# A 64-channel remainder as 64-row matmuls in pairs, in a backward pass of 18 weight groups

## The chip, the cores and the metric

The kernel runs on one core of one Trainium2 chip. The metric is device time in microseconds (us) of one execution. The engines are TensorE (PE; its weight loads are PEld), VectorE (DVE), ScalarE (ACT), GpSimd (POOL) and SyncE (SP, which here only issues DMAs). Each executes its own instructions strictly in the order in which the program lists them.

## What is computed

The program is a layer and its gradients: `x + s * g` with a long convolution `s` (through Fourier transforms) and a gated feed-forward block `g`, and from `grad_out` the gradients of all inputs. L = 2048 tokens, D = 576 channels, F = 4608 hidden channels, bfloat16.

```
def _B_ref(x, w1, w3, w2):
    gate = jnp.einsum("bsd,df->bsf", x, w1)
    up = jnp.einsum("bsd,df->bsf", x, w3)
    h = _silu(gate) * up
    out = jnp.einsum("bsf,fd->bsd", h, w2)
    return out
...
xn = _layernorm(x, axis=-1)
s = _A_ref(xn, ...)            # y = irfft(rfft(u) * rfft(K)) + u * Dskip
g = _silu(_B_ref(xn, B_w1, B_w3, B_w2))
return x + s * g
```

The change concerns one product of the backward pass: the gradient by `h`, which is `go @ w2^T` with `go` the gradient by the feed-forward block's output (2048 x 576) and w2 (4608 x 576). Its inner dimension is D = 576 = 4 x 128 + 64.

## The kernel before

F is cut into 18 groups of 256 columns (`gi` 0 to 17), which run from about 645 to 1330 us; tokens are cut into 16 tiles of 128. In each group:

- `phase6_group` makes the gradient by `h` in four steps `s`. A step serves four token tiles: tiles 2s and 2s+1 of the first eight (j = 0) and the same of the last eight (j = 1), with one PSUM bank `ph` (pool `ps_h`, three banks) for each j. A tile takes five matmuls of 256 columns (L1936), one for each piece of 128 channels of `goT` against `w2T`. The fifth piece is `goTt`, whose rows 0 to 63 hold the 64 channels that remain and whose rows 64 to 127 are zero; `w2rows` is padded with zeros alike (L1690), and its transpose `w2T` comes by DMA (L1851). That is 80 matmuls in a group, 1440 in all, 288 of them the padded ones.
- ACT copies each bank to `gh` (L1939), and DVE multiplies `gh` into `gu_n` and `gg_n` (L1954: two products in a step, eight in a group).
- `phase6_grad2` makes the gradient by w2 (L1977, copies by ACT in L1983), `phase6_grad13` the gradients by w1 and w3 from `gu_n`, `gg_n` and `xn_bf` (L2002, then the 64 channels that remain as pairs of column halves in L2011 and L2013). `phase6_prep` prepares the next group on ACT (silu and its derivative, each with a table load) and DVE (L1900, L1901).

Beside groups 0 to 10 runs the backward convolution (`ssm_bwd_conv`): transforms on PE (L932), products of complex blocks on DVE (L963 to L971, into `Z`), the combination of two blocks into `ZZ` (L1453 on DVE), the inverse transform of `ZZ` on PE (L942, 16 matmuls for one ZZ, into two banks of the pool `et_ps` with three banks), scaled out of the banks by ACT and DVE (`gk_st`, L1470, L1473); and a second kind, from `Z` straight through PE (L952) with `gx` from ACT and DVE (L1500 to L1502). From group 11 on the parameter gradients take the convolution's place (L1537 on PE into `et_ps`, L1542 and L1545 on DVE).

The order on each engine is fixed when the program is built: the code emits operations with a due time (`self.at(us)`), and a scheduler picks by priority among those that are ready in its own reckoning. ACT's, SP's and POOL's operations of the groups are chained in the order in which they are emitted (`self.sc`, `self.sp`, `self.gp`). Pools hand out their banks in the order of the program too.

Of the kernel before, what the change touches and what calls it, by code (L numbers as in the profile page):

```python
# [13 lines left out]
FP32 = mybir.dt.float32  # L14
# [3 lines left out]
P = 128  # L18
# [82 lines left out]
class K:  # L101
    LEAD, SPAN, KG, TURN, TWICE = 1, 38, (4, 6.9), 34, 8
    SYNC = 13
    BACK = ((49, 0), (54, 0), (64, 2), (69, 1))

# [1056 lines left out]
    def ffn_output(self, T0, TB):  # L1162
# [9 lines left out]
        with ExitStack() as es:  # L1172
# [107 lines left out]
            def turn(i, after):  # L1280
                self.turn_go(i, pst.tile([P, DT, P], BF16, name="ptr"), after)

# [8 lines left out]
            product(second, F0, FT, last)  # L1291
            nc.gpsimd.memset(goTt[rem:P, :], 0.0)
            finish(first)
# [11 lines left out]
    def turn_go(self, i, ptr, after=None):  # L1305
        nc, cfg = self.nc, self.cfg
        nfull, rem = cfg.D // P, cfg.D % P
        for c, (do, dsz) in enumerate(cfg.dch):
            with self.tc.issue_after(after.ins) if after is not None else nullcontext():
                nc.tensor.transpose(ptr[0:dsz, c, :], self.go_o[:, i, do:do + dsz], self.ident_bf[:])  # L1310
        nc.scalar.copy(out=self.goT[:, :, i * P:(i + 1) * P], in_=ptr[:, 0:nfull, :])
        nc.scalar.copy(out=self.goTt[0:rem, i * P:(i + 1) * P], in_=ptr[0:rem, nfull, :])

# [67 lines left out]
    def conv_bwd_quarter(self, g, kp, zp, ps, T0, TQ):  # L1381
# [38 lines left out]
        for b in range(NB - 1, -1, -1) if g else range(NB):  # L1420
            self.at(T0 + (TQ * 0.05 * (NB - 1 - b) if g else 0))
            after = None
            if g == 0 and b == NB - 1:
                pt = ps.tile([P, 512], FP32, name="et_ps")
                self.turn_go(LT - 1, pt[:].bitcast(BF16)[:, 0:cfg.DT * P].rearrange("p (c t) -> p c t", t=P), self.dft_last)
                yield
                self.at(T0)
                after = self.pe_last
            G[b] = self.bgp.tile([P, 1, 2, KT, W], BF16, name=f"g_{b}")
            if g == 0:  # L1430
                folded = fold(slice(b, b + 1))
            if g == 0 and b == 0:
                after = first
            with self.tc.issue_after(after.ins) if after is not None else nullcontext():
                self.dft_folded(ps, self.cCS, (sums[b], gm[:, b]), G[b])
            if g == 0 and b == NB - 1:
                yield
# [225 lines left out]
    def backward(self, T0, TG, TQ, TC, TX, gctx, mats):  # L1663
# [11 lines left out]
        with ExitStack() as out:  # L1675
# [12 lines left out]
            self.w2rows = [rowp.tile([P, self.FG // P, cfg.DT * P], BF16, name=f"w2r{i}") for i in range(2)]  # L1688
            for w2r in self.w2rows:
                nc.gpsimd.memset(w2r[:, :, D:cfg.DT * P], 0.0)  # L1690
            with self.tc.issue_after(self.hc_loads[7].ins):
# [22 lines left out]
            self.at(T0)  # L1714
            group = self.phase6_group(0, cur, elp, gwp, ps_h, ps_gw)
            next(group)
# [32 lines left out]
            for gi in range(NG):  # L1749
# [9 lines left out]
                w2 = lambda g, fl: self.phase6_grad2(g, fl, hs[g], gwp, ps_gw)  # L1759
                for stage in group if gi == 0 else self.phase6_group(gi, cur, elp, gwp, ps_h, ps_gw):  # L1760
                    if stage == "h3" and self.chain and gi + 2 < NG:
# [63 lines left out]
    def w2row_load(self, gi):  # L1825
        D = self.cfg.D
        nfl = self.FG // P
        for fl in range(nfl):
            fi = gi * nfl + fl
            self.sp(lambda: self.nc.sync.dma_start(out=self.w2rows[gi % 2][:, fl, 0:D],  # L1830
                                                   in_=self.aps["B_w2"][fi * P:(fi + 1) * P, :]))

# [80 lines left out]

    def phase6_group(self, gi, tiles, elp, gwp, ps_h, ps_gw):
        nc, cfg = self.nc, self.cfg
# [4 lines left out]
        pair = lambda t_: t_[:].rearrange("p (j t) f -> p j t f", j=2)  # L1920
        made = {}

        def make(s):
            if gi == 0 and s == 3:
                gh = gwp.tile([P, 2, 2, FG], BF16, name="gh_3", tag="gw13")
            else:
                gh = elp.tile([P, 2, 2, FG], BF16, name="gh6")
            ph = [ps_h.tile([P, 2, FG], FP32, name="ph") for _ in range(2)]
            for k in range(2):
                t = s * 2 + k  # L1930
                for j in range(2):
                    tt = j * LH + t
                    steps = [(self.goT[:, c, tt * P:(tt + 1) * P], w2T[:, :, c, :]) for c in range(nfull)]
                    steps.append((self.goTt[:, tt * P:(tt + 1) * P], w2T[:, :, nfull, :]))
                    for n, (lw, rh) in enumerate(steps):
                        self.pe_last = nc.tensor.matmul(ph[j][:, k, :].rearrange("p (a f) -> p a f", f=P), lhsT=lw, rhs=rh,  # L1936
                                                        start=(n == 0), stop=(n == nfull))
            for j in range(2):
                self.sc(lambda: nc.scalar.copy(out=gh[:, j], in_=ph[j][:]))  # L1939
            made[s] = gh  # L1940
# [363 lines left out]
```

## Time and profile before

| what | value |
|---|---|
| three runs | 1632.05, 1639.41, 1641.4 us (median 1639.41) |
| span of the profiled execution | 1639.1 us |
| busy PE, DVE, ACT, POOL in that span | 1568.0, 1384.4, 837.0, 516.6 us |
| L1936, the product | 1440 matmuls, mean 273 ns of one |
| L1939, the bank copies | 144, mean 588 ns |

Times in the rows are us from the span's start. A row of a timeline has the start, the time until the last of its instructions ends, the engine, the line, out<-in, rows*columns of the weights, the tile's shape and the number of instructions that follow one another; in brackets the idle time before them and what ended it. Matmuls overlap, so a matmul's own duration (about 0.27 us here) is more than the distance from one to the next. A row of a table by stretches gives the stretch and its length, then busy us of PE, PEld, DVE, ACT and POOL with their instructions, the granted TensorE clock (1.00 is full speed), the DMA share and GB/s. A row of groups gives busy us and the mean ns of one after the bar, then the idle time before them with what ended most of it.

### The profile page before, as it was taken

To read this page: it belongs to the slowest core of one execution; us is meant where nothing else is said; L and a number is where in the kernel's file an instruction comes from. 1 tells how busy PE (TensorE), PEld (TensorE's weight loads), DVE (VectorE), ACT (ScalarE), POOL (GpSimd) and SP (SyncE) were. 2 spreads that over 40 slices of the span, in tenths; PEclk is the share of its full clock that TensorE was granted. 3 is DMA by queue.
4 is the path that set the end of the run, shared out by engine and by line. 5 is a ranking of instruction groups with operands and counts; after the bars stand their busy time and mean duration, and the time that the engine had idled before them with its cause. 6 is when DMAs were issued, how large, how long until landed. Compare 5 with 4: busy or idle time off the path is not lost. (4 is left out here: it accounts for less than half of the span.)

```text
span 1639.1 us, 34391 instructions
## 1 busy us (share of the span) xinstructions
PE 1568.0 (96%) x13331; PEld 1145.2 (70%) x13331; DVE 1384.4 (84%) x2145; ACT 837.0 (51%) x1520; POOL 516.6 (32%) x862
## 2 busy tenths in 40 slices
PE   6899999999999998999999999999999999999998
PEld 2454444444457776788888888888888887888786
DVE  8889998799965664998997999789999963988797
ACT  6989998766652114656556565565555411010011
POOL 7746765632352110111111011112122341515232
PEclk9999999999999999999999999999999999999999
DMA  7999999998999999676585766899999999999994
GB/s 236 346 345 363 374 346 382 369 268 257 320 287 214 240 200 205 182 216 202 176 246 156 213 190 183 226 240 264 247 272 223 244 254 241 240 216 215 237 241 88
DMA packets 616156, 408.26 MB, mean 249 GB/s; under 512 B 424698, under 2 KB 558426, under 8 KB 611386
## 3 DMA queue, kind: packets, MB, share of 16 engines
q1 hardware_dynamic: 561232, 277.45, 68.5%
q0 software_dynamic: 36576, 116.69, 22.2%
q10 hardware_dynamic: 18186, 11.95, 2.5%
q8 instruction: 104, 1.70, 0.4%
q14 instruction: 58, 0.48, 0.1%
HBM read 128.52 MB, written 188.76 MB: 194 GB/s over the span
## 5 line engine op out<-in xcount | busy, mean ns | idle before, releaser
L2002 PEld LDWEIGHTS <-xn_bf 128*128 128x128 bf16 x2304 | 224.3, 98 | 34.9 <-issue 8.7
L2056 PEld LDWEIGHTS <-acts 128*128 128x128 bf16 x1974 | 191.5, 98 | 52.3 <-DMA acts<-GG_dram 3.1
L1987 POOL DMA_DIRECT2D out_dram<-gw x72 | 47.2, 656 | 530.0 <-ACT gw L2004 313.8
L1542 DVE TENSOR_TENSOR pr_q<-et_ps,pz 128x1024 f32<-128x1024 f32 x144 | 175.8, 1221 | 28.7 <-PE et_ps L1537 21.0
L1123 PEld LDWEIGHTS <-xnT 128*128 128x128 bf16 x1152 | 107.9, 98 | 127.9 <-issue 20.9
L1545 DVE TENSOR_REDUCE S_all<-pr_q 128x32 f32<-128x1024 f32 x144 | 175.2, 1216 | 3.3
L1936 PE MATMUL ph<-w2T,goT 128*128 128x256 bf16 x1440 | 169.7, 273 | 1.5 <-ACT gh L1939 1.4
L1123 PE MATMUL pg<-wmB_w,xnT 128*128 128x512 bf16 x576 | 156.7, 381 | 1.1 <-DVE g_t L1142 0.6
L1977 PE MATMUL pgw<-go_o,h_n 128*128 128x288 bf16 x1152 | 152.4, 286 | 1.3 <-ACT gw L1983 1.0
L1936 PEld LDWEIGHTS <-goT 128*128 128x128 bf16 x1440 | 139.2, 98 | 18.7 <-issue 2.9
L1123 PE MATMUL pu<-wmB_w,xnT 128*128 128x512 bf16 x576 | 149.7, 379 | 0.0
L2056 PE MATMUL px<-wT,acts 128*128 128x288 bf16 x1134 | 145.8, 286 | 0.0
L2002 PE MATMUL pgw<-gu_n,xn_bf 128*128 128x256 bf16 x1152 | 133.3, 272 | 3.8 <-ACT gw L1983 3.3
L1977 PEld LDWEIGHTS <-h_n 128*128 128x128 bf16 x1152 | 111.9, 98 | 29.2 <-issue 2.1
L2002 PE MATMUL pgw<-gg_n,xn_bf 128*128 128x256 bf16 x1152 | 130.3, 273 | 0.4 <-ACT gw L2004 0.4
L1939 ACT CAST gh<-ph 128x512 bf16<-128x512 f32 x144 | 80.3, 588 | 82.9 <-PE ph L1936 76.5
L1138 ACT ACTIVATE s_t<-pg 128x512 bf16<-128x512 f32 x144 | 88.5, 614 | 55.8 <-PE pu L1132 43.2
L2179 ACT ACTIVATE go<-gx 128x576 bf16<-128x576 f32 x15 | 10.2, 683 | 195.3 <-DVE gx L2127 189.0
L813 POOL COPY KT<-k_s 64x128 bf16<-64x128 bf16 x144 | 84.5, 587 | 54.2 <-ACT k_s L810 49.5
L2056 PE MATMUL px<-wA,acts 128*128 128x288 bf16 x728 | 95.4, 286 | 4.4 <-DMA acts<-GG_dram 2.5
L1143 ACT CAST u_t<-pu 128x512 bf16<-128x512 f32 x144 | 87.5, 608 | 6.3 <-PE pu L1123 6.2
L1152 POOL DMA_DIRECT2D G_dram<-g_t x72 | 51.4, 715 | 119.0 <-ACT g_t L1140 91.1
(338 smaller groups left out, 3236.7 us busy)
## 6 DMA issues: line engine op xcount, KB each, us to landing
U_dram<-u_t POOLq DMA_DIRECT2D x72, 256.0 KB, 6.2
H_dram<-h_t SPq DMA_DIRECT2D x72, 256.0 KB
G_dram<-g_t POOLq DMA_DIRECT2D x72, 256.0 KB, 5.7
Q_dram<-q_k SPq DMA_DIRECT2D x36, 512.0 KB
GG_dram<-gg_n SPq DMA_DIRECT2D x36, 512.0 KB
GU_dram<-gu_n SPq DMA_DIRECT2D x36, 512.0 KB
gg_n<-G_dram POOLq DMA_DIRECT2D x14, 1024.0 KB, 6.6
E_dram<-E_k SPq DMA_DIRECT2D x54, 256.0 KB
```

The costliest lines, as they stand in the source:

```text
L813: nc.gpsimd.tensor_copy(out=KT[64 * hf:64 * hf + 64, :, ch // 9, h, d1:d1 + 8], in_=ks[64 * h:64 * h + 64, :, h, hf].rearrange("p d a -> p ...
L1123: ins = nc.tensor.matmul(pt[:], lhsT=xnT[:, c, ts], rhs=wm[w][:, c, :], start=(q == 0 and c == 0), stop=(q == 1 and c == nfull - 1))
L1138: nc.scalar.activation(out=s_t[:, :, q, :], in_=pgv, func=ACT.Silu)
L1143: self.gate_last = nc.scalar.copy(out=u_t[:, :, q, :], in_=puv)
L1152: self.u_stores[step] = nc.gpsimd.dma_start(out=dst[fb * ng:(fb + 1) * ng, :, i0:i0 + NT, :].rearrange("g p t f -> p g (t f)"), in_=src[:] ...
L1542: nc.vector.tensor_tensor(out=pr[:].rearrange("p r k e -> p r (k e)"), in0=T[x][:].rearrange("p z k h j a -> p (z k h j a)")[:, None].to_b ...
L1545: self.pr_last = nc.vector.tensor_reduce(out=self.S_all[:].rearrange("p r (h c) -> p r h c", h=2)[:, :, :, d0:d0 + 2], in_=pr[:].rearrange ...
L1936: self.pe_last = nc.tensor.matmul(ph[j][:, k, :].rearrange("p (a f) -> p a f", f=P), lhsT=lw, rhs=rh, start=(n == 0), stop=(n == nfull))
L1939: self.sc(lambda: nc.scalar.copy(out=gh[:, j], in_=ph[j][:]))
L1977: self.pe_last = nc.tensor.matmul(pgw[pi_][:, 0:pw], lhsT=hn[:, tt, fl * P:(fl + 1) * P], rhs=go_o[:, tt, po:po + pw], start=(tt == 0), st ...
L2002: self.pe_last = nc.tensor.matmul(pw_[:, 0:FG], lhsT=self.xn_bf[:, tt, c * P:(c + 1) * P], rhs=nat[:, tt, :], start=(tt == 0), stop=(tt == ...
L2056: self.pe_last = nc.tensor.matmul(px[pi_][:, 0:pw], lhsT=acts[i][:, ai, fi, :], rhs=w[:, po:po + pw], start=(n == 0), stop=(n == len(steps ...
```

## The change

The token tiles of j = 0 keep their 64 remaining channels in rows 0 to 63 of `goTt`, those of j = 1 go to rows 64 to 127, and the 64 channels of w2 are loaded twice, into both halves of the last piece of `w2rows`. The padded matmul becomes one of 64 rows, and the two of a pair (j = 0 and j = 1) use the two halves of the rows. The three memsets of zeros go; each `w2rows` block takes two DMAs instead of one (36 more on SP). In 15 groups two steps are made together: full pieces of the first tile of step s, those of step s+1, then four pairs of tails, then the full pieces of the second tiles. That needs four banks at a time: three `ph` and one `et_ps`. Groups 0, 2 and 8 (`LONE`) make each step alone, with two pairs in a run. `turn_go` puts the transposed tail, now a matmul with the identity, into its half of the rows.

```diff
@@ class K @@
+    LONE = (0, 2, 8)
...
-            nc.gpsimd.memset(goTt[rem:P, :], 0.0)
...
@@ -1305,11 +1305,16 @@
     def turn_go(self, i, ptr, after=None):
         nc, cfg = self.nc, self.cfg
         nfull, rem = cfg.D // P, cfg.D % P
-        for c, (do, dsz) in enumerate(cfg.dch):
-            with self.tc.issue_after(after.ins) if after is not None else nullcontext():
-                nc.tensor.transpose(ptr[0:dsz, c, :], self.go_o[:, i, do:do + dsz], self.ident_bf[:])
-        nc.scalar.copy(out=self.goT[:, :, i * P:(i + 1) * P], in_=ptr[:, 0:nfull, :])
-        nc.scalar.copy(out=self.goTt[0:rem, i * P:(i + 1) * P], in_=ptr[0:rem, nfull, :])
+        half, t = divmod(i, cfg.LT // 2)
+        r = slice(rem * half, rem * half + rem)
+        full = ptr[:].bitcast(BF16)[:, 0:nfull * P].rearrange("p (c t) -> p c t", t=P)
+        tail = ptr[r, 256:256 + P]
+        with self.tc.issue_after(after.ins) if after is not None else nullcontext():
+            for c in range(nfull):
+                nc.tensor.transpose(full[:, c, :], self.go_o[:, i, c * P:(c + 1) * P], self.ident_bf[:])
+            nc.tensor.matmul(tail, lhsT=self.go_o[:, i, nfull * P:cfg.D], rhs=self.ident_bf[:], start=True, stop=True)
+        nc.scalar.copy(out=self.goT[:, :, i * P:(i + 1) * P], in_=full)
+        nc.scalar.copy(out=self.goTt[r, t * P:(t + 1) * P], in_=tail)
 
     def ssm_bwd_conv(self, T0, TQ, ps):
         nc, cfg = self.nc, self.cfg
...
-            for w2r in self.w2rows:
-                nc.gpsimd.memset(w2r[:, :, D:cfg.DT * P], 0.0)
...
@@ -1827,8 +1830,9 @@
         nfl = self.FG // P
         for fl in range(nfl):
             fi = gi * nfl + fl
-            self.sp(lambda: self.nc.sync.dma_start(out=self.w2rows[gi % 2][:, fl, 0:D],
-                                                   in_=self.aps["B_w2"][fi * P:(fi + 1) * P, :]))
+            for o, d in ((0, 0), (D, D - D % P)):
+                self.sp(lambda: self.nc.sync.dma_start(out=self.w2rows[gi % 2][:, fl, o:o + D - d],
+                                                       in_=self.aps["B_w2"][fi * P:(fi + 1) * P, d:D]))
 
     def load_piece(self, wT, pool, tag, ai, f0, n):
         t = pool.tile([P, n, self.cfg.D], BF16, name=f"wT{ai}_{f0}", tag=tag)
@@ -1911,32 +1915,57 @@
                 products(sl)
             yield
 
-    def phase6_group(self, gi, tiles, elp, gwp, ps_h, ps_gw):
+    def phase6_group(self, gi, tiles, elp, gwp, ps_h, ps_gw, ps_b):
         nc, cfg = self.nc, self.cfg
         D, LT, FG = cfg.D, cfg.LT, self.FG
         nfull = D // P
         LH = LT // 2
         w2T, hn, gg, gu = tiles[0:4]
         pair = lambda t_: t_[:].rearrange("p (j t) f -> p j t f", j=2)
-        made = {}
+        made, phs = {}, {}
+        pairs = gi not in self.LONE
+        rem = D % P
+
+        def banks(s):
+            pools = (ps_h, "ph"), (ps_b, "et_ps") if pairs and s % 2 else (ps_h, "ph")
+            phs[s] = [pool.tile([P, 2, FG], FP32, name=name) for pool, name in pools]
+
+        def put(s, j, k, lhsT, rhs, start, stop, after):
+            with self.tc.issue_after(after.ins) if after is not None else nullcontext():
+                self.pe_last = nc.tensor.matmul(phs[s][j][:, k, :].rearrange("p (a f) -> p a f", f=P), lhsT=lhsT, rhs=rhs,
+                                                start=start, stop=stop)
+
+        def fulls(s, k, after):
+            for j in range(2):
+                tt = j * LH + s * 2 + k
+                for c in range(nfull):
+                    put(s, j, k, self.goT[:, c, tt * P:(tt + 1) * P], w2T[:, :, c, :], k == 0 and c == 0,
+                        k == 1 and c == nfull - 1, after if c == 0 else None)
+                after = self.pe_last
+
+        def tails(s, k):
+            t = s * 2 + k
+            for j in range(2):
+                r = slice(rem * j, rem * j + rem)
+                put(s, j, k, self.goTt[r, t * P:(t + 1) * P], w2T[r, :, nfull, :], k == 1, k == 0, self.pe_last)
 
         def make(s):
             if gi == 0 and s == 3:
                 gh = gwp.tile([P, 2, 2, FG], BF16, name="gh_3", tag="gw13")
             else:
                 gh = elp.tile([P, 2, 2, FG], BF16, name="gh6")
-            ph = [ps_h.tile([P, 2, FG], FP32, name="ph") for _ in range(2)]
+            run = (s, s + 1) if pairs and s % 2 == 0 else () if pairs else (s,)
+            after = None
+            for r in run:
+                banks(r)
+                fulls(r, 0, after)
+                after = self.pe_last
             for k in range(2):
-                t = s * 2 + k
-                for j in range(2):
-                    tt = j * LH + t
-                    steps = [(self.goT[:, c, tt * P:(tt + 1) * P], w2T[:, :, c, :]) for c in range(nfull)]
-                    steps.append((self.goTt[:, tt * P:(tt + 1) * P], w2T[:, :, nfull, :]))
-                    for n, (lw, rh) in enumerate(steps):
-                        self.pe_last = nc.tensor.matmul(ph[j][:, k, :].rearrange("p (a f) -> p a f", f=P), lhsT=lw, rhs=rh,
-                                                        start=(n == 0), stop=(n == nfull))
+                for r in run:
+                    tails(r, k)
+            fulls(s, 1, self.pe_last)
             for j in range(2):
-                self.sc(lambda: nc.scalar.copy(out=gh[:, j], in_=ph[j][:]))
+                self.sc(lambda: nc.scalar.copy(out=gh[:, j], in_=phs[s][j][:]))
             made[s] = gh
 
         if gi == 0:
```

The other edits pass the pool `ps` (the banks `et_ps`) to `phase6_group` and a bank of fp32 to `turn_go`. Line numbers of the changed kernel are higher: L1936 becomes L1935, L1939 L1968, L1954 L1983, L1977 L2006, L1983 L2012, L2002 L2031, L942 L943, L952 L953, L1453 L1458, L1473 L1478.

How the order changes is seen best in group 1. On PE of the kernel before, the ZZ with number 9300 is first read behind the group's last gradients (`pgw`, L2011 and L2013); `[waits DVE_49]` marks a wait for DVE:

```order
L2011 LDWEIGHTS xn_bf_103
L2011 MATMUL pgw_10008<-gg_n_9353,xn_bf_103 64x256
L2013 LDWEIGHTS xn_bf_103
L2013 MATMUL pgw_10008<-gu_n_9355,xn_bf_103 64x256
L942 LDWEIGHTS iT_6076
L942 MATMUL et_ps_9306<-ZZ_9300,iT_6076 128x144 [waits DVE_49]
```

All 80 matmuls of L1936 and the gradients of group 1 stand ahead of these rows. On PE of the changed kernel the same ZZ (now 9301) is read in two single matmuls ahead of group 1's first run, whose bank `et_ps_9671` is the first row of L1935 there:

```order
L943 MATMUL et_ps_9263<-ZZ_9246,iT_6076 128x144
L943 LDWEIGHTS iT_6076 [waits DVE_49]
L943 MATMUL et_ps_9307<-ZZ_9301,iT_6076 128x144 [waits PE_49]
L943 LDWEIGHTS iT_6076
L943 MATMUL et_ps_9321<-ZZ_9301,iT_6076 128x144 [waits PE_49]
L1935 LDWEIGHTS goT_6965
L1935 MATMUL et_ps_9671<-w2T_8883,goT_6965 128x256 [waits PE_49]
```

So the wait for that ZZ moved from behind group 1's work on PE to ahead of its 80 matmuls; the other 14 matmuls of that ZZ follow behind the product and the gradients. On DVE of the kernel before, the first products of group 1 (`gh6_9654`, `gh6_9681`) stand around the ZZ before that one (9245):

```order
L922 TENSOR_TENSOR gk_x_9246<-Z_9225,Z_9184 128x576
L1954 TENSOR_TENSOR gu_n_9355<-gh6_9654,gu_n_9355 128x2x512
L1453 TENSOR_TENSOR ZZ_9245<-gk_x_9246 128x2x288 x2
L1954 TENSOR_TENSOR gg_n_9353<-gh6_9654,gg_n_9353 128x2x512
L1954 TENSOR_TENSOR gu_n_9355<-gh6_9681,gu_n_9355 128x2x512
L1473 TENSOR_TENSOR gk_st_9152<-et_ps_9251,lcol_8931 128x18x8x2
L1954 TENSOR_TENSOR gg_n_9353<-gh6_9681,gg_n_9353 128x2x512
```

On DVE of the changed kernel the first product of group 1 (`gh6_9659`, L1983) stands behind the ZZ 9301, with nine rows of the next convolution block between:

```order
L970 TENSOR_TENSOR cm_t_10112<-g_2_9004,a2_0_9336 128x1152
L1458 TENSOR_TENSOR ZZ_9301<-gk_x_9302 128x2x288 x2
L964 TENSOR_TENSOR Z_9344<-g_3_9126,a2_0_9336 128x1152
L964 TENSOR_TENSOR Z_10110<-g_2_9004,a2_0_9336 128x1152
L971 TENSOR_TENSOR Z_9344<-Z_9344,cm_t_9346 128x576
L972 TENSOR_TENSOR Z_9344<-Z_9344,cm_t_9346 128x576
L971 TENSOR_TENSOR Z_10110<-Z_10110,cm_t_10112 128x576
L972 TENSOR_TENSOR Z_10110<-Z_10110,cm_t_10112 128x576
L967 TENSOR_TENSOR cm_t_10116<-g_3_9126,a2_1_9338 128x1152
L970 TENSOR_TENSOR cm_t_10119<-g_3_9126,a2_1_9338 128x1152
L968 TENSOR_TENSOR Z_10110<-Z_10110,cm_t_10116 128x1152
L1983 TENSOR_TENSOR gu_n_9358<-gh6_9659,gu_n_9358 128x2x512
```

All eight products of group 1 moved 27 rows or more down DVE's list, behind that ZZ. Groups 3 and 5 change in the same way: in group 3 the matmuls of two ZZ and the first two of a third, in group 5 the whole inverse transform of the next phase (34 matmuls of L943) stand ahead of the runs.

More of the change, by code (lines that the diff above doesn't have):

```diff
@@ L1280, in turn @@
             def turn(i, after):
-                self.turn_go(i, pst.tile([P, DT, P], BF16, name="ptr"), after)
+                self.turn_go(i, pst.tile([P, 512], FP32, name="ptr"), after)
             first = begin(0)
@@ L1424, in conv_bwd_quarter @@
                 pt = ps.tile([P, 512], FP32, name="et_ps")
-                self.turn_go(LT - 1, pt[:].bitcast(BF16)[:, 0:cfg.DT * P].rearrange("p (c t) -> p c t", t=P), self.dft_last)
+                self.turn_go(LT - 1, pt, self.dft_last)
                 yield
@@ L1714, in backward @@
             self.at(T0)
-            group = self.phase6_group(0, cur, elp, gwp, ps_h, ps_gw)
+            group = self.phase6_group(0, cur, elp, gwp, ps_h, ps_gw, ps)
             next(group)
@@ L1759, in backward @@
                 w2 = lambda g, fl: self.phase6_grad2(g, fl, hs[g], gwp, ps_gw)
-                for stage in group if gi == 0 else self.phase6_group(gi, cur, elp, gwp, ps_h, ps_gw):
+                for stage in group if gi == 0 else self.phase6_group(gi, cur, elp, gwp, ps_h, ps_gw, ps):
                     if stage == "h3" and self.chain and gi + 2 < NG:
```

## The prediction

> **What bounds the kernel now.** I read the page's busy times first, then the table by stretches, then the timelines of TensorE (PE) and VectorE (DVE) where the convolution runs beside the groups.
>
> ```profile
> span 1639.1 us, 34391 instructions
> ...
> PE 1568.0 (96%) x13331; PEld 1145.2 (70%) x13331; DVE 1384.4 (84%) x2145; ACT 837.0 (51%) x1520; POOL 516.6 (32%) x862
> L1936 PE MATMUL ph<-w2T,goT 128*128 128x256 bf16 x1440 | 169.7, 273 | 1.5 <-ACT gh L1939 1.4
> L2002 PE MATMUL pgw<-gu_n,xn_bf 128*128 128x256 bf16 x1152 | 133.3, 272 | 3.8 <-ACT gw L1983 3.3
> ...
> 700.00:740.00 40.00, 39.08 (x388) 33.90 (x386) 38.35 (x71) 22.86 (x40) 4.79 (x8) 1.00 0.76 217
> 860.00:900.00 40.00, 39.25 (x389) 33.73 (x388) 27.84 (x49) 25.19 (x48) 4.78 (x8) 1.00 0.52 160
> ```
>
> PE is the bound: 96% of the span, nearly all of these stretches (second number of a row). Less PE work could thus show in the time. But DVE is almost as full (38.35 of 40 us around 720). Whatever makes PE wait for DVE there costs directly, and the schedule of before is one in which PE always has other work while DVE computes.
>
> **The tails themselves.** The gate stage shows pairs of 64-row matmuls in this kernel, the plain column is L1936's run of 40 in group 1 (below).
>
> ```profile
> 303.20 0.81 PE L1123 MATMUL pu<-wmB_w,xnT 128*128 128x512 bf16 x3
> 303.94 0.39 PE L1132 MATMUL pg<-wtail,xnT 64*128 64x512 bf16 x1
> 304.17 0.38 PE L1132 MATMUL pg<-wtail,xnT 64*128 64x512 bf16 x1
> 304.48 0.29 PE L804 MATMUL kps<-v_k,q_k 128*128 128x64 bf16 x4
> ```
>
> Three full 512-column matmuls start at 303.20 and take 0.81 with a last one of about 0.38, so their pitch is 0.215 and the last starts at 303.63. The pair starts 0.31 later (0.097 over the pitch), the next pair 0.23 after it, and full rows 0.31 after that (again 0.096 over). With L1936's pitch of 0.109 ((4.53 - 0.273)/39 in the 40 matmuls at 696.14), a run of four pairs takes 0.206 + 3 x 0.120 + 0.205 = 0.77 from the last full start to the next, where eight padded matmuls and the next full one took 9 x 0.109 = 0.98: 0.21 saved. A run of two pairs takes 0.53 against 0.55. Thirty runs of four and twelve of two (groups 0, 2 and 8) give -6.6 us of PE at most.
>
> The Trainium skill ("TensorEngine Tiling (Array Packing)", Key Properties) says that a change of tiling mode drains TensorE, which speaks against short runs. Were each of the 84 switches to wait for the 0.38 that a row above lasts rather than 0.31, the saving would shrink by 84 x 0.07 = 5.6 us, to about 1; the starts above show a switch cheaper than that.
>
> How much of it is kept? Group 14 shows what ends a group's second run:
>
> ```profile
> 1193.72 1.09 ACT L1939 CAST gh<-ph 128x512 bf16<-128x512 f32 x2 [1.10 <-PE ph L1936]
> 1194.83 1.28 ACT L1904 ACT_TABLE_LOAD   x1
> 1197.08 0.38 ACT L1983 CAST gw<-pgw 128x288 bf16<-128x288 f32 x1
> ...
> 1197.52 0.71 PE L2002 MATMUL pgw<-gu_n,xn_bf 128*128 128x256 bf16 x5 [0.27 <-ACT gw L1983]
> ```
>
> The gradients (L2002) already wait for a ScalarE (ACT) chain: last gh copies, table load, silu, gw copy. After the change the four banks of steps 2 and 3 close together, so four copies of about 0.55 stand in a row behind the run and the chain does not start earlier. I give the second run of a group nothing and the first its 0.21: **-3 us**, between -6.6 (all kept) and 0.
>
> **Small parts.** Out go three POOL memsets (POOL is 32% busy and nobody waits: 0). The 16 tail transposes become matmuls of one row with the same number of columns, in a stage where PE waits for DMA: 0, within half a us. The 36 extra SP transfers stand in front of others in SP's queue; they matter where PE waits for SP's loads, at 632.89 (row below, 4.41 us): **+1**, between 0 and another 4.4.
>
> **The order, the large term.** A run now needs a fourth bank, which comes from et_ps, the pool that the convolution's inverse transform (L942, L943 after) uses. On PE all 80 matmuls of groups 1, 3 and 5 move behind that transform's first matmuls for the next operand ZZ (made by DVE, L1453), and with them everything behind: copies, DVE's gh products (L1954), gradients. Group 1 before:
>
> ```profile
> 692.28 0.30 PE L942 MATMUL et_ps<-ZZ,iT 128*128 128x144 bf16 x2
> 692.95 1.03 PE L942 MATMUL et_ps<-ZZ,iT 128*128 128x144 bf16 x14
> 696.14 4.53 PE L1936 MATMUL ph<-w2T,goT 128*128 128x256 bf16 x40
> 700.51 3.23 PE L1977 MATMUL pgw<-go_o,h_n 128*128 128x288 bf16 x25
> 704.00 1.91 PE L2002 MATMUL pgw<-gu_n,xn_bf 128*128 128x256 bf16 x16 [0.27 <-ACT gw L1983]
> 721.44 0.74 PE L942 MATMUL et_ps<-ZZ,iT 128*128 128x144 bf16 x9
> ...
> 692.81 0.68 DVE L1954 TENSOR_TENSOR gg_n<-gh,gg_n 128x1024 bf16<-128x1024 bf16 x1
> 693.41 0.68 DVE L1954 TENSOR_TENSOR gu_n<-gh,gu_n 128x1024 bf16<-128x1024 bf16 x1
> 710.60 1.42 DVE L1453 TENSOR_TENSOR ZZ<-gk_x 128x576 bf16<-128x576 f32 x2
> ...
> L1954 DVE TENSOR_TENSOR gg_n<-gh,gg_n 128x1024 bf16<-128x1024 bf16 x4 | 2.7, 683 | 0.0
> L1954 DVE TENSOR_TENSOR gu_n<-gh,gu_n 128x1024 bf16<-128x1024 bf16 x3 | 2.0, 682 | 0.0
> ```
>
> The last two rows group DVE's products from 692.5 to 703.5. DVE finishes the ZZ in question at 710.60 + 1.42 = 712.0, and PE needs it only at 721.44. After, that ZZ has no product ahead of it: seven at a pitch of 0.60 (692.81 to 693.41) fall out, 4.2 us, so its rows run from 706.4 to 707.8. PE gets there at about 694.5 (the 16 matmuls of L942 end at 692.95 + 1.03, a few of L1977 come with them) and has nothing else to issue: it waits some **12 us**. Then it does the two L943 (0.1), 80 matmuls with two runs (8.3) and 26 of L1977's kind (3.2), and the ACT chain takes its 0.3: the gradients start 11.9 later, at 719.7 instead of 704.00: **+15** (rounded down, since an eighth product moves behind as well). DVE cannot use the time: its next convolution rows need PE's L952 results of group 2, which are 15 later too.
>
> Group 3 is built alike; its third ZZ of the phase now stands ahead of the runs.
>
> ```profile
> 766.03 0.82 DVE L1453 TENSOR_TENSOR ZZ<-Z 128x576 bf16<-128x576 bf16 x2
> 789.68 1.42 DVE L1453 TENSOR_TENSOR ZZ<-gk_x 128x576 bf16<-128x576 f32 x2
> 783.12 1.91 PE L2002 MATMUL pgw<-gu_n,xn_bf 128*128 128x256 bf16 x16 [0.27 <-ACT gw L1983]
> ...
> L1954 DVE TENSOR_TENSOR gu_n<-gh,gu_n 128x1024 bf16<-128x1024 bf16 x4 | 2.7, 681 | 0.0
> L1954 DVE TENSOR_TENSOR gg_n<-gh,gg_n 128x1024 bf16<-128x1024 bf16 x4 | 2.7, 680 | 0.0
> ```
>
> From 766.03 to 789.68 DVE also does the group's eight products (last two rows, 766 to 789), 4.8 us at 0.60; without them the third ZZ comes 18.8 after the first, at 784.9 by the old clock, which is 15 late by now: 799.9. Two rows (1.4) and 11.9 later the gradients start, 813.2, 30 after 783.12: another **+15**.
>
> Group 5 takes the next phase's whole transform (34 matmuls of L943) ahead of its runs, which before lay in group 6:
>
> ```profile
> 850.44 1.16 PE L952 MATMUL et_ps<-Z,cT 128*128 128x144 bf16 x16 [0.91 <-DVE Z L970]
> 857.83 0.83 DVE L1453 TENSOR_TENSOR ZZ<-Z 128x576 bf16<-128x576 bf16 x2
> 858.50 0.71 PE L2002 MATMUL pgw<-gu_n,xn_bf 128*128 128x256 bf16 x5 [0.27 <-ACT gw L1983]
> ...
> 940.39 0.82 PE L2002 MATMUL pgw<-gu_n,xn_bf 128*128 128x256 bf16 x6 [0.18 <-ACT gw L1983]
> 1161.98 1.19 PE L2002 MATMUL pgw<-gu_n,xn_bf 128*128 128x256 bf16 x8 [0.27 <-ACT gw L1983]
> ```
>
> The first ZZ hangs on transforms behind the L952 at 850.44, 30 late: 887.8. The third follows 18.8 later (group 3's spacing), 906.6; plus 1.4 and 11.9 the gradients start at 919.9 instead of 858.50: 61 late, another **+30**. Some of it comes back: from 858.50 to 940.39 two groups took 81.9 us with that transform between them; without it group 6 is a plain one, and I take **-9**, between 0 and -11 (twice a group without convolution, 35.5 from 1161.98 to 1197.52). In groups 7 and 10 the L952 waits (0.91 at 850.44) lose the matmuls of L1936 that stood ahead of them, some 50 x 0.109 = 5.5 each, of which DVE, freed of a few products, gives back a part: **+7**, between 0 and 11. Laid end to end with these durations through PE, ACT and DVE, the rest of the groups shift alike.
>
> **The clock after a long wait.**
>
> ```profile
> 632.89 3.29 PE L1248 MATMUL po<-w2g,hcA 128*128 128x288 bf16 x16 [4.41 <-DMA hcA<-H_dram]
> 635.97 3.42 PE L1248 MATMUL po<-w2a,hcA 128*128 128x288 bf16 x22
> 639.23 0.56 PE L1310 MATMUL ptr<-ident_bf,go_o 128*128 128x128 bf16 x5
> ...
> 633.00:635.00 2.00, 2.00 (x12) 1.34 (x11) 0.00 (x0) 0.00 (x0) 0.00 (x0) 0.67 0.96 394
> 635.00:637.00 2.00, 2.00 (x10) 1.27 (x9) 0.99 (x2) 0.23 (x1) 0.00 (x0) 0.50 0.93 238
> ```
>
> After 4.41 us idle the granted clock (last but two) falls to 0.50 until 637, and the 38 matmuls take 6.34 us, where L1977's pitch ((3.23 - 0.286)/24 = 0.123) gives 4.66: 1.7 us lost. Of the long waits above four (groups 1, 3, 5, 10) have no further wait behind them that swallows it: **+7**, between 0 and twice that.
>
> **Sum:** -3 + 1 + 15 + 15 + 30 - 9 + 7 + 7 = +63. The profiled execution spans 1639.1 us, the median of three runs is 1639.41, so the same base: **1702 us**.
>
> **Rivals.**
> - *Only the first wait costs* (13 in 100). DVE's room between 860 and 900 (27.84 of 40 busy) says that it can run ahead; if the later ZZ are ready when PE comes, +15, the clock's 2 and the Z waits' 7 stay, less 3, plus 1: 1661. Against it: DVE's first rows of each phase need PE's results, so it is late with PE.
> - *More is late than PE and DVE* (12). The convolution's operands also come by DMA, which the walk takes as ready. A wait as at 632.89 (4.41 and 1.7) in each of five phases, once or twice, gives +30 to +60: 1730 to 1760.
> - *No wait: DVE has ZZ before PE asks, and the whole saving shows* (3). It decides from the point where DVE brings ZZ by 695 instead of 706, with under 3 us of its rows between the two ZZ, not 14. All runs then end early, the ACT chain with them, and L2002's 3.3 us of waits go as well: 1639.4 - 6.6 - 3.3 = 1629.5, faster by 0.6%.
> - *The change does little: runs' saving eaten by chain and banks, the order neutral* (4). 1639.4 - 3 + 1 = 1637.
>
> **How the numbers follow.** The forecast has 68 in 100, its own range 1672 to 1722: each group term may be a third smaller or the clock and Z terms double. Reaching down to the first rival's middle and a little over the top, 1660 to 1726 leaves out two in ten. A change under 0.5% (8 us, about what a measurement of this kernel can tell) needs the third or fourth rival: faster 0.02, same 0.05, slower 0.93.
>
> **What would show it.** Right: a wait of PE of 10 us or more in front of the runs in groups 1, 3 and 5, ended by DVE's ZZ row; granted clock near a half in the 3 us behind; L2031 at about 719, 813 and 920; groups from 12 on at the pace of before; pairs' members started together, 0.2 before and after. Wrong: PE busy through the runs of group 1, gradients there before 710, or DVE's ZZ row long done when PE arrives. The forecast falls if PE's instructions are not executed in the order shown, or if DVE's work between two ZZ is far shorter than the trace has them.

## The result, and the profile after

The changed kernel takes 1723.2 us in the median of four runs (1711.6 to 1740.5), the kernel before 1640.4: 1.048 times as long, 95% interval 1.043 to 1.053. Later runs on another occasion gave 1713.4 us and 1.042 (1.036 to 1.049). Ratios and their intervals, here and below, leave out the executions that lie over 1.5% above the fastest of the same kernel, among them that of the first profile of the changed kernel (1740.5 us), while the medians keep them. The first profile of the changed kernel spans 1738.7 us, the second 1702.5; where they differ is part of the explanation.

The page's head and the view of what TensorE waited for (us in total, times, longest), first profile:

```profile
span 1738.7 us, 34424 instructions
PE 1580.6 (91%) x13331; PEld 1133.7 (65%) x13331; DVE 1390.8 (80%) x2145; ACT 834.0 (48%) x1520; POOL 515.3 (30%) x859
...
PE et_ps L943 <- DVE ZZ L1458: 44.3, 11, 12.6
PE po L1249 <- DMA hcA<-H_dram: 28.6, 2, 27.9
PE et_ps L953 <- DVE Z L971: 14.5, 4, 5.2
```

PE's share fell from 96% to 91%, with nearly the same work. Three waits grew by 75.5 us together, most of the 99.6 us by which the span is longer: the inverse transform's for ZZ (2.7 us before), that for the load hcA ahead of group 0 (5.4 before, the longest piece 4.4), and the second transform's for Z (3.8 before). The timeline of PE in group 1, and the two ZZ rows of DVE:

```profile
717.83 0.30 PE L943 MATMUL et_ps<-ZZ,iT 128*128 128x144 bf16 x2
718.49 1.04 PE L943 MATMUL et_ps<-ZZ,iT 128*128 128x144 bf16 x14
732.11 0.42 PE L943 MATMUL et_ps<-ZZ,iT 128*128 128x144 bf16 x2 [12.59 <-DVE ZZ L1458]
732.33 1.06 PE L1935 MATMUL et_ps<-w2T,goT 128*128 128x256 bf16 x4
...
741.16 3.35 PE L2006 MATMUL pgw<-go_o,h_n 128*128 128x288 bf16 x26
744.81 1.91 PE L2031 MATMUL pgw<-gu_n,xn_bf 128*128 128x256 bf16 x16 [0.30 <-ACT gw L2012]
...
717.02 1.42 DVE L1458 TENSOR_TENSOR ZZ<-gk_x 128x576 bf16<-128x576 f32 x2
731.31 1.42 DVE L1458 TENSOR_TENSOR ZZ<-gk_x 128x576 bf16<-128x576 f32 x2
```

PE stands still from 719.5 to 732.1, until DVE has the next ZZ, then does the product (all but its first twelve matmuls, which came earlier) and only then the gradients. Counted from the last rows of group 0 (683.46 before, 709.0 after), the gradients of group 1 start at 35.8 instead of 20.5.

The distance of a group's first L2011 (L2040) from that of the group ahead, from the timelines, in us:

| group | before | changed, first profile | changed, second | difference (first) |
|---|---|---|---|---|
| 1 | 36.1 | 51.3 | 51.5 | +15.2 |
| 2 | 37.7 | 37.9 | 37.9 | +0.2 |
| 3 | 41.4 | 57.3 | 57.3 | +15.9 |
| 4 | 37.3 | 37.5 | 37.5 | +0.2 |
| 5 | 38.1 | 69.0 | 69.0 | +30.9 |
| 6 | 44.7 | 35.0 | 35.0 | -9.7 |
| 7 | 36.8 | 41.5 | 41.5 | +4.7 |
| 8, 9 | 42.0, 37.8 | 41.6, 39.5 | 41.6, 39.5 | +1.3 |
| 10 | 37.4 | 42.0 | 42.0 | +4.6 |
| 12 to 15 | 35.5 each | 35.7, 36.9, 35.7, 35.7 | 35.7, 35.7, 35.7, 36.7 | +0.2 each, two with a DMA wait |

Groups 1 to 10 together are 63.3 us longer. Where group 0's first of these rows lies is another matter: 683.5 before, 709.0 in the first profile, 683.2 in the second.

### The profile page after: what moved, and what is told of

It reads as the page before. It is cut to its first block, busy times and chain, and to the rows that moved or that the text cites. A ratio compares the mean times of both kernels' runs of the same rounds, so it can differ in the third digit from the quotient of the medians.

```text
span 1738.7 us, 34424 instructions
## 1 busy us (share of the span) xinstructions
PE 1580.6 (91%) x13331; PEld 1133.7 (65%) x13331; DVE 1390.8 (80%) x2145; ACT 834.0 (48%) x1520; POOL 515.3 (30%) x859
## 5 line engine op out<-in xcount | busy, mean ns | idle before, releaser
L2031 PEld LDWEIGHTS <-xn_bf 128*128 128x128 bf16 x2304 | 224.4, 98 | 36.7 <-issue 10.5
L1547 DVE TENSOR_TENSOR pr_q<-et_ps,pz 128x1024 f32<-128x1024 f32 x144 | 176.0, 1222 | 43.5 <-PE et_ps L1542 36.1
L2006 PE MATMUL pgw<-go_o,h_n 128*128 128x288 bf16 x1152 | 151.9, 286 | 2.3 <-DVE h_n L1905 1.4
L1935 PEld LDWEIGHTS <-goT 128*128 128x128 bf16 (+1 forms) x1440 | 122.2, 100 | 37.5 <-issue 21.8
L1935 PE MATMUL ph<-w2T,goT 128*128 128x256 bf16 (+1 forms) x1140 | 142.1, 281 | 0.6 <-ACT gh L1968 0.6
L2031 PE MATMUL pgw<-gu_n,xn_bf 128*128 128x256 bf16 x1152 | 133.0, 272 | 5.5 <-ACT gw L2012 4.0
L2006 PEld LDWEIGHTS <-h_n 128*128 128x128 bf16 x1152 | 111.9, 98 | 29.8 <-DVE h_n L1905 1.8
L2031 PE MATMUL pgw<-gg_n,xn_bf 128*128 128x256 bf16 x1152 | 130.3, 273 | 0.4 <-ACT gw L2033 0.4
L1968 ACT CAST gh<-ph 128x512 bf16<-128x512 f32 x114 | 60.7, 592 | 120.7 <-PE ph L1935 120.5
L1904 DVE TENSOR_TENSOR gg_n<-gg_n,h_n 128x1024 bf16<-128x1024 bf16 x72 | 48.7, 685 | 50.1 <-ACT gg_n L1911 48.2
```

Source lines behind the costliest of these rows:

```text
L1547: nc.vector.tensor_tensor(out=pr[:].rearrange("p r k e -> p r (k e)"), in0=T[x][:].rearrange("p z k h j a -> p (z k h j a)")[:, None].to_b ...
L1904: nc.vector.tensor_tensor(out=gg[:, sl, :], in0=gg[:, sl, :], in1=hn[:, sl, :], op=ALU.mult)
L1935: self.pe_last = nc.tensor.matmul(phs[s][j][:, k, :].rearrange("p (a f) -> p a f", f=P), lhsT=lhsT, rhs=rhs, start=start, stop=stop)
L1968: self.sc(lambda: nc.scalar.copy(out=gh[:, j], in_=phs[s][j][:]))
L2006: self.pe_last = nc.tensor.matmul(pgw[pi_][:, 0:pw], lhsT=hn[:, tt, fl * P:(fl + 1) * P], rhs=go_o[:, tt, po:po + pw], start=(tt == 0), st ...
L2031: self.pe_last = nc.tensor.matmul(pw_[:, 0:FG], lhsT=self.xn_bf[:, tt, c * P:(c + 1) * P], rhs=nat[:, tt, :], start=(tt == 0), stop=(tt == ...
```

## Experiments

The runs test two theories: (1) the loss has two causes, the place of the inverse transform ahead of the runs (some 60 us) and the extra SP transfers ahead of the hcA load; (2) rivals to each: the 64-row runs themselves are dear, a run over two steps is late whatever its banks, the later waits are absorbed, the hcA wait is chance.

### The changed kernel once more

> The changed kernel once more, for a profile of another execution and a closer ratio. Theory 1 (two causes): the waits of PE for ZZ in groups 1, 3 and 5 are 12.6, 3.9 + 9.0 and 6.6 + 9.0 us in every execution, since they follow from the order; the wait for the hcA load ahead of group 0 (27.9 us in the first profile, 4.4 before) differs from run to run, and makes the spread from 1711 to 1740. Rival: the waits in the groups vary too, because DMA is behind them.

1713.4 us, 1.042 (1.036 to 1.049). The waits for hcA, and those for ZZ and Z between 660 and 1200 us:

```profile
PE po L1249 <- DMA hcC<-H_dram: 2.8, 1, 2.8
PE po L1249 <- DMA hcA<-H_dram: 2.5, 1, 2.5
...
PE et_ps L943 <- DVE ZZ L1458: 44.3, 11, 12.6
PE et_ps L953 <- DVE Z L971: 14.5, 4, 5.2
```

The ZZ and Z waits are the same to the last digit shown; single ones (12.59, 3.9, 8.95, 5.16, 6.65, 8.95) agree within 0.01 us. The hcA wait went from 27.9 to 2.5. So the waits for DVE come with the order of the instructions, and the wait for hcA changes from execution to execution.

### Two-pair runs everywhere, no shared bank

```diff
-    LONE = (0, 2, 8)
+    LONE = tuple(range(18))
```

> All 18 groups make each step alone (runs of two pairs, only ph banks); the doubled w2 rows and the 36 extra SP transfers stay. Theory 1: the order of before is back in the convolution, PE's waits for ZZ fall under 2 us, and what stays is the wait for hcA: 1645 to 1665 us. Rival (the short 64-row runs themselves cost, each switch of TensorE dearer than the 0.1 us seen): 36 more two-pair runs than the changed kernel has, 1690 us or more, and the groups without convolution slower than 35.5 us.

1664.6 us in the median, with ten executions from 1638.6 to 1680.6; 1.0064 (1.0015 to 1.0114). The waits between 660 and 1200 us, and that for hcA in this and in a second profile (told of further below):

```profile
PE et_ps L953 <- DVE Z L971: 4.2, 6, 0.9
PE et_ps L943 <- DVE ZZ L1458: 2.6, 6, 0.6
...
PE po L1249 <- DMA hcA<-H_dram: 33.9, 1, 33.9
...
PE po L1249 <- DMA hcA<-H_dram: 18.3, 1, 18.3
```

All 18 groups use 64-row pairs here, in 72 runs of two (60 more than in the changed kernel, not the 36 expected above), and the distances of groups 1 to 10 are those of before within half a us (35.8, 38.0, 41.7, 37.4, 38.1, 44.7 for groups 1 to 6). The rows' tiling is not what costs; the order is. What stays is, in the main, the hcA wait.

### The extra transfers alone

```diff
-            self.sp(lambda: self.nc.sync.dma_start(out=self.w2rows[gi % 2][:, fl, 0:D],
-                                                   in_=self.aps["B_w2"][fi * P:(fi + 1) * P, :]))
+            for o, d in ((0, 0), (D, D - D % P)):
+                self.sp(lambda: self.nc.sync.dma_start(out=self.w2rows[gi % 2][:, fl, o:o + D - d],
+                                                       in_=self.aps["B_w2"][fi * P:(fi + 1) * P, d:D]))
...
-            for w2r in self.w2rows:
-                nc.gpsimd.memset(w2r[:, :, D:cfg.DT * P], 0.0)
```

> The kernel before with the 36 extra SP transfers alone (the last 64 channels of w2 twice, against the zero rows of go). Theory 1: the wait for hcA grows from 4.4 to 15 or more, 1650 to 1665 us, everything else as before. Rival (the hcA wait of the changed kernel comes from its other edits ahead of group 0, such as the tail transposed by a matmul, or from chance): 1640 us, wait under 6.

1653.8 us, 1.0043 (1.0008 to 1.0079): in the expected range, though the wait in its profile, 11.0 us, is shorter than expected. A second profile of the same kernel:

> A second profile of the kernel before with all 36 extra transfers, for the wait at hcA (11.0 us in the first). Theory: it varies from run to run, between 2 and 35 us, and mostly lies over that of the kernel before. Rival: it is a fixed 11.

```profile
PE po L1248 <- DMA hcA<-H_dram: 11.0, 1, 11.0
...
PE po L1248 <- DMA hcA<-H_dram: 14.5, 1, 14.5
```

So the kernel before, with nothing but these transfers (and without the memsets, which the runs with a copy below leave out as well, without a wait), waits 11.0 and 14.5 us where it waited 4.4. The second profile of two-pair runs and one of before:

> A second profile of two-pair runs everywhere with the extra transfers (wait at hcA 33.9 us in the first). Theory: varies, 2 to 35 us. Rival: 33.9 again.

18.3 us (shown above).

> A second profile of the kernel before (wait at hcA 4.4 us in the first). Theory: under 8 us, the rest of the profile alike. Rival: it varies as much without the extra transfers, up to 30 us, and the extra transfers are innocent.

No wait for hcA there. Over all profiles: with the extra transfers ahead 27.9, 2.5, 33.9, 18.3, 11.0, 14.5 (mean 18); without them 4.4 once and none in seven others. The wait varies, but it belongs to these transfers. The profiles with the longest waits, 27.9 and 33.9, are of executions of 1740.5 and 1680.6 us, those with 2.5 and 11.0 of executions of 1704.4 and 1650.1.

The SP queue shows where the time sits. Rows of the changed kernel (first profile), of before, and of the kernel with two-pair runs and a copy (told of below): start, the time until SP had handed over the transfer, and the start of a load of 1024 KB, gg_n, that POOL issues:

```profile
613.13 0.57 SPq L1834 DMA_DIRECT2D w2r<-in_B_w_dram  x1
614.24 1.00 SPq L1834 DMA_DIRECT2D w2r<-in_B_w_dram  x2
615.84 25.95 SPq L1855 DMA_TRANSPOSE hcA<-H_dram  x1
617.04 0.53 POOL L1859 DMA_DIRECT2D gg_n<-G_dram  x1 [2.08 <-PE po L1249]
...
613.11 7.05 SPq L1851 DMA_TRANSPOSE hcA<-H_dram  x1
617.16 0.53 POOL L1855 DMA_DIRECT2D gg_n<-G_dram  x1 [1.96 <-PE po L1248]
...
612.92 5.62 SPq L1854 DMA_TRANSPOSE hcA<-H_dram  x1
620.89 0.54 POOL L1858 DMA_DIRECT2D gg_n<-G_dram  x1 [2.09 <-PE po L1249]
```

The load hcA starts 2.7 us later on SP with the extra transfers in this pair of profiles, but then takes 26 us to hand over instead of 7. All fourteen profiles fall into three classes, without overlap in the first column:

| kernels | handing over hcA, us | gg_n starts behind the start of hcA by, us |
|---|---|---|
| all extra transfers (six profiles) | 11.7 to 39.5 | 0.9 to 3.4 |
| none, or from group 4 on only (three) | 7.1, 9.3, 9.5 | 4.1, 5.6, 7.3 |
| copy in their place (five) | 5.6 to 5.7 | 7.5 to 8.2 |

Why a few transfers of 16 KB slow the transposing load so much was not settled, and two rivals stand. One is what is directly ahead of it: of the eight w2 loads of groups 2 and 3, three (two of 16 KB, one of 144 KB) come between the load hcC and hcA here, where without the extra ones all four stand ahead of hcC. The five ahead of hcC do not slow that one (4.9 to 9.2 us to hand over in six profiles, 5.3 to 9.5 in the eight others). The other is gg_n: hcA is 2.7 us later and gg_n is not, so the two loads run side by side from near their start, and gg_n too takes longer to land (33.5 us in the first profile, 15.9 before, 5.8 with the copy). Within the six profiles the handing over does not follow the distance between the two, and no run changes the one without the other.

### Extra transfers from group 4 on only

```diff
-            for o, d in ((0, 0), (D, D - D % P)):
+            for o, d in ((0, 0), (D, D - D % P))[:2 if gi >= 4 else 1]:
```

(against the run with all extra transfers; the memsets are back)

> The kernel before with the extra SP transfers from group 4 on only (28 of the 36), so that none stands ahead of the hcA load that PE waits for before group 0. Theory (those few ahead of hcA are the loss of 7 to 10 us): time as before within 0.3%, wait for hcA under 6. Rival (the other extra transfers, beside the groups, cost too): 0.4% slower as with all 36.

1642.9 us, 1.0008 (0.9968 to 1.0049), no wait for hcA in its profile. The eight extra transfers ahead of hcA (two of them directly ahead) are the costly ones by this, the 28 beside the groups cost nothing measurable. By time alone the two kernels are not told apart, since the intervals overlap (that with all 36 was 1.0008 to 1.0079).

### A copy in place of the extra transfers

```diff
-            for o, d in ((0, 0), (D, D - D % P)):
-                self.sp(lambda: self.nc.sync.dma_start(out=self.w2rows[gi % 2][:, fl, o:o + D - d],
-                                                       in_=self.aps["B_w2"][fi * P:(fi + 1) * P, d:D]))
+            self.sp(lambda: self.nc.sync.dma_start(out=self.w2rows[gi % 2][:, fl, 0:D],
+                                                   in_=self.aps["B_w2"][fi * P:(fi + 1) * P, :]))
...
+        w2r, D = self.w2rows[gi % 2], self.cfg.D
+        self.nc.gpsimd.tensor_copy(out=w2r[:, :, D:self.cfg.DT * P], in_=w2r[:, :, D - D % P:D])
```

(the copy stands in `phase6_load_w2`, ahead of the transposes)

> The changed kernel with the doubled w2 rows filled by a GpSimd copy inside SBUF in place of the extra SP transfers. Theory 1: the wait for hcA is back under 6 us, the waits for ZZ stay: 1690 to 1705 us. Rival: as the changed kernel, 1711 to 1740.

1698.8 us, 1.035 (1.029 to 1.041), no wait for hcA, the waits for ZZ as before this edit (44.3 us in eleven pieces). With the copy, the four-pair kernel loses the order's part alone: 1698.8 - 1643.7 (before, same occasion) = 55 us, some 9 less than groups 1 to 10 are longer in its profile (64.0). What makes up the 9 us was not looked into. The copy does one thing more: POOL waits 8.4 us for the w2 load that it copies from (in the profile of the next run), so that gg_n starts only when hcA has been handed over. This run therefore does not tell the extra transfers from gg_n as the cause of the hcA wait.

### Two-pair runs with the copy

> Runs of two pairs in every group, the doubled rows by the GpSimd copy: 64-row tails without the shared bank and without the extra SP transfers. Theory (order and SP transfers are the whole loss, two-pair runs pay nothing): as before within 0.3%, no wait for hcA over 5 us, groups without convolution at 35.5 us. Rival (64-row runs bring a cost of their own): 0.5% slower or more.

1639.4 us, 0.9987 (0.9953 to 1.0021): no difference from before. Both parts of the loss are gone and nothing measurable is left over; nor does the change then save anything.

### Four-pair runs in groups 11 to 17 only

```diff
-    LONE = (0, 2, 8)
+    LONE = tuple(range(11))
```

(with the copy)

> As the run with two-pair runs and the copy, but groups 11 to 17, which have no convolution beside them, take four-pair runs with the et_ps bank. Theory of the prediction (the second run of a group gives its saving to the ACT chain, and the et_ps bank is late by 0.1 to 0.2 us in the first): groups 12 to 16 take 35.5 to 35.7 us, time as with two-pair runs alone. Rival (the saving of 0.2 us for each run shows): 35.1 us a group, some 3 us off the time.

1643.5 us, 0.9999 (0.9962 to 1.0035); groups 12 to 15 take 35.7 us each, 35.4 with two-pair runs (where no DMA wait falls in), 35.5 before. The saving does not show; these groups are 0.2 to 0.3 longer. PE in one of them:

```profile
1177.16 1.47 PE L1936 MATMUL ph<-w2T,goT 128*128 128x256 bf16 x12
1178.66 0.60 PE L1936 MATMUL et_ps<-w2T,goT 128*128 128x256 bf16 x4
1179.19 0.39 PE L1936 MATMUL ph<-w2T,goT 64*128 64x256 bf16 x3
1179.74 1.49 PE L1936 MATMUL ph<-w2T,goT 128*128 128x256 bf16 x12
...
1193.65 0.81 PE L2032 MATMUL pgw<-gu_n,xn_bf 128*128 128x256 bf16 x6 [0.30 <-ACT gw L2013]
1194.81 1.25 PE L2032 MATMUL pgw<-gu_n,xn_bf 128*128 128x256 bf16 x10 [0.34 <-DVE gu_n L1984]
```

Four full matmuls start at 1178.66, so the last at 1178.99; the run of four pairs begins 0.20 later and the next full one starts at 1179.74: 0.75 us where the prediction had 0.77. The run is as cheap as reckoned. But the `et_ps` bank comes 0.19 late in the first run (12 x 0.109 = 1.31 after 1177.16 is 1178.47), and behind the second run the gradients wait for ACT as before and then once more for DVE's last products, since the last two steps' products now come together.

### Only group 1 with four-pair runs

```diff
-    LONE = (0, 2, 8)
+    LONE = tuple(g for g in range(18) if g != 1)
```

(with the copy)

> Only group 1 takes the four-pair runs with the et_ps bank, the rest two-pair runs, doubled rows by the copy. Theory (a wait for ZZ shifts everything behind it, since DVE's next rows need PE): the group takes 51.5 us instead of 36, one wait of 12.6 us, and all of it stays to the end: 15 us over the run with two-pair runs everywhere. Rival (DVE uses the lead and PE gets it back in the next groups): groups 2 to 6 are shorter than in the kernel before by several us, less than 8 us stay.

1662.5 us, 1.011 (1.006 to 1.016), some 20 over before and 23 over two-pair runs alone, where 15 were expected. In its profile group 0 ends 5 us later than with two-pair runs alone (its first L2041 at 687.7 against 682.5), which this edit doesn't explain; group 1 takes 50.9 us against 35.8, with one wait:

```profile
711.08 0.42 PE L943 MATMUL et_ps<-ZZ,iT 128*128 128x144 bf16 x2 [12.58 <-DVE ZZ L1458]
```

Groups 2 to 10 take 37.9, 41.7, 37.4, 38.1, 44.7, 36.8, 41.5, 38.3, 37.3 against 38.0, 41.7, 37.4, 38.1, 44.7, 36.8, 41.5, 38.3, 37.4 with two-pair runs alone. The 15 us stay to the last one; nothing is absorbed. Of the 8 us by which the time exceeds the expectation, these 5 are the only part found.

### Four banks of their own

```diff
-            ps_h = ffn.enter_context(pool(name="e_ps_h", bufs=3, space=PS, side="right"))
+            ps_h = ffn.enter_context(pool(name="e_ps_h", bufs=4, space=PS, side="right"))
...
-            ps = out.enter_context(pool(name="b_ps", bufs=3, space=PS))
+            ps = out.enter_context(pool(name="b_ps", bufs=2, space=PS))
...
-            pools = (ps_h, "ph"), (ps_b, "et_ps") if pairs and s % 2 else (ps_h, "ph")
+            pools = (ps_h, "ph"), (ps_h, "ph")
```

(with the copy, four-pair runs in 15 groups)

> The four-pair runs in 15 groups as in the change, but with four banks of their own (ph 4, et_ps 2 instead of 3 and 3) and the copy. Theory (the shared pool, which hands out its banks in the order of the program, put the inverse transform ahead of the runs): no wait for ZZ of over 3 us in groups 1, 3 and 5, and the time within 1% of before, since et_ps has a bank less. Rival (a run over two steps is late whatever its banks, since copies and DVE's products come later with it): waits of PE of 10 us stay, 1690 us.

1650.2 us, 1.0036 (1.0008 to 1.0065). PE's waits between 683 and 960 us, then between 1060 and 1300:

```profile
PE et_ps L953 <- DVE Z L971: 2.8, 4, 1.2
PE et_ps L943 <- DVE ZZ L1458: 1.5, 3, 0.7
...
PE et_ps L1542 <- DVE pr_q L1547: 6.8, 5, 1.4
```

No wait for ZZ of over 0.7 us: with its own banks the same run over two steps stands among the transform's matmuls as before. The shared pool is what moved the transform ahead. What is left goes with the third `et_ps` bank that is missing: groups 12 to 15 take 36.5 us each, with waits of L1542 for DVE, which releases a bank.

## Why the prediction held, term by term

1702 us was forecast, range 1660 to 1726; 1723.2 and 1713.4 were measured, and the second profile, in which hcA came early, spans 1702.5. As a ratio the forecast is 1.038, and 1.048 and 1.042 were measured. That one execution meets it within a us is luck: two terms were off, each by more than that.

- **The order: right in mechanism and size.** Forecast +15 in group 1, +15 in group 3, +30 in group 5, -9 in group 6, +7 in groups 7 and 10, +7 for the clock: 65. Measured for groups 1 to 10: +63.3, group by group 15.2, 15.9, 30.9, -9.7, 4.7 and 4.6. In the second profile, in which these rows of group 0 lie as before (683.2 and 683.5), the gradients of groups 1, 3 and 5 start at 719.3, 814.5 and 920.9; 719, 813 and 920 were named. The waits ahead of the runs are 12.6 in group 1, 3.9 and 8.95 in group 3, 6.65 and 8.95 in group 5, each ended by DVE's ZZ row. Those of groups 3 and 5 stay under the 10 us that the prediction named as the sign, since each group waits for two ZZ in turn.
- **The clock after a wait: right, in size too.** In group 1 the granted clock (last but two) stays at 0.50 for some 4 us behind the wait, first profile:

```profile
728.00:732.00 4.00, 0.00 (x0) 0.00 (x0) 3.97 (x8) 0.00 (x0) 0.00 (x0) 0.50 0.26 74
732.00:734.00 2.00, 1.89 (x14) 1.11 (x14) 2.00 (x5) 0.00 (x0) 0.00 (x0) 0.50 0.00 0
734.00:736.00 2.00, 2.00 (x13) 1.22 (x10) 2.00 (x6) 0.58 (x1) 0.00 (x0) 0.50 0.03 8
736.00:738.00 2.00, 2.00 (x18) 1.74 (x17) 2.00 (x4) 1.79 (x4) 0.00 (x0) 0.92 0.00 0
```

  The product there took 8.8 us (732.33 to 741.16) where its 68 matmuls need 7.0 at full speed (68 x 0.109 less two savings of 0.21): 1.8 lost, the 1.7 forecast. The same 68 took 9.2 us in group 3 (827.18 to 836.37) and 8.6 in group 5 (934.28 to 942.84), 2.2 and 1.6 lost, and in group 10 the clock was at 0.50 for some 3 us of PE's work, of which half is lost by an estimate from these rows, 1.5: 7.1 together, where 7 was forecast. Not foreseen are stretches at 0.50 behind the waits for Z in group 5 (4.4 us of PE's work) and group 7 (3.1); how much of them later waits swallow was not measured. Nor did the prediction see that only 68 of the 80 matmuls stand behind the wait: the first twelve, in `ph` banks, are ahead of it, 12 x 0.109 = 1.3 us. So group 1 took 15.2 more where 15 and 1.7 for the clock were forecast.
- **Extra SP transfers: the term that was mis-sized.** Forecast +1, bounded by another 4.4 us. With the transfers ahead the wait for hcA was 2.5 to 33.9 us, 18 in the mean of six profiles; as time, the copy in their place takes the ratio from 1.042 to 1.035 (some 12 us, but the intervals overlap, 1.036 to 1.049 and 1.029 to 1.041), and the transfers alone cost 0.43% (7 us, interval 1 to 13). The step that failed took the transfers as a place in SP's queue (they do set hcA back by 2.7 us) and not the time that the load behind them then takes: 11.7 to 39.5 us to hand over, against 5.6 to 9.5. Whether the transfers themselves or the collision with gg_n slow it stays open. The row in the trace of before that could have warned is that load itself: 7.05 us to hand over, and PE waited 4.41 us for it later.
- **The pairs' saving: the price of a run was right (0.75 against 0.77), the sum was not.** Forecast -3; no time shows any of it. The run with two-pair runs, which by the reckoning saves nothing, is level with before, and four-pair runs in the last groups are 0.2 to 0.3 us a group longer. The first run's 0.2 went to the late bank, the second's to the ACT chain and DVE's last products; the prediction had told the second only.
- **The rivals.** That only the first wait costs: refuted, groups 3 and 5 wait 12.8 and 15.6 us for ZZ and are 15.9 and 30.9 us longer. That the convolution's transfers are late too: refuted for the groups, whose waits repeat within 0.01 us; transfers were late, but ahead of group 0. That the order is neutral, or that the saving shows: refuted. Drains at each change of tiling, which the Trainium skill has in "TensorEngine Tiling (Array Packing)", Key Properties: 72 two-pair runs make 144 such changes and leave no loss that can be measured (0.9987, 0.9953 to 1.0021), and the starts show 0.20 us from the last full matmul to the first pair, less than the 0.27 that the rows give a matmul of 256 columns.

## What to carry to other kernels

Ask of a change what it takes from a pool that others use: a bank borrowed for 0.2 us a run tied the product to the transform that holds the pool's other banks, and PE, which ran the rows in the order listed, waited 59 us for VectorE (44.3 for ZZ and 14.5 for Z) instead of 6.5. Walk the new order with the old durations at the places where an engine that was always ahead becomes one that is waited for; that walk, not the count of instructions, gave the time here. And price a transfer not by its own size alone: look at the load behind it in its queue, and at what else is under way when that load starts.

## What the runs showed of the hardware that was not expected

A large transposing load took 5.6 to 39.5 us to hand over in fourteen profiles, with the same bytes each time. It took 11.7 us or more in all six in which eight extra transfers of 16 KB (rows of 128 bytes) stand ahead of it, two of them directly, and in which a load of 1024 KB from POOL starts within 3.4 us of it; PE then waited 2.5 to 33.9 us. It took 7.1 to 9.5 us where that load starts 4.1 to 7.3 us behind it, and 5.6 to 5.7 where it starts after the handing over. Which of the two slows it is not shown. The 28 extra transfers elsewhere in the queue cost nothing that could be measured.

A change of tiling cost little: 0.20 us from a full matmul's start to that of the first 64-row pair, some 0.1 us over the pitch of 0.109.
